# Two token groups turned in 64-token halves, seven taps one by one, token rows cut as 0–127 and 64–191

## The chip, the cores and the metric

The kernel runs on one core of a Trainium2 chip. The metric is device time in microseconds (us); the profile below is of one execution on that core. Its engines are TensorE (PE, with its weight loads PEld), VectorE (DVE), ScalarE (ACT), GpSimd (POOL) and the DMA queues that SyncE (SP) issues.

## The reference

Tokens `x` (4 × 4096 × 192) go through a dynamic convolution of 7 taps with softmax weights, 8 heads of 24 columns each, and then through a gated two-layer network with 1536 hidden columns.

```
w = softmax(weight_gen, over the 7 taps)          # per token and head
attn[s, h, :] = sum_k w[s, h, k] * x_pad[s + k, h, :]      # k = 0..6, causal
out = (silu(attn @ w_gate) * (attn @ w_val)) @ w_out       # 192 -> 1536 -> 192
```

Inputs are float32 but the arrays arrive as 64-bit floats, so the three weight matrices are rebuilt from their bits on DVE and ACT inside the kernel.

## The kernel before

The 16384 tokens are 32 groups of 4 × 128 (`NG`, `JG`; `NC` = 512 tokens). A step is one group and one of 12 slices of 128 hidden columns; groups 0 and 1 are worked in alternate steps so that the first weight slices, which are still being rebuilt, are used twice; groups 2 to 31 follow in turn. Before a group's first step its summed tokens must stand with the 192 columns on partitions. A partition has 128 rows, so the 192 are held in two tiles: `xT[g, 0]` holds rows 0–127, and `xT[g, 1]` rows 128–191, twice over (partitions 0–63 and 64–127). In the program tile 1 is "half 1". Each is split for accuracy into a rounded part (`xhi`, made by ACT, `high`) and the rest (`xlo`, by DVE, `low`).

Groups 2 to 31 (`MOVED`) are turned through DRAM. Groups 0 and 1 are needed at once, and are turned on TensorE (`summed_turn`): a matmul takes 128 tokens × 128 columns of a tap as the stationary operand and the identity as the moving one, and adds into two PSUM banks, one a half. The seven taps of a token are put together as five sums (`SUMS`): pairs (3,4) and (5,6) are added on DVE first (`product`, the line with `op=ALU.add`), the others go alone; one tap is multiplied on ACT (`scaled`, 32 small activations of 24 columns). For half 1 to be doubled, ACT copies the last 64 columns behind the 192 (the activations with `out=x[:, :, D:]`: L340, and L369 in `doubled`). So a sum costs eight matmuls of 128 × 128, two halves by four token blocks. A float32 matmul stands in the trace as two records.

An up-projection takes nine pairs of matmuls of 64 rows (`up_first`, L587 and L590, `up_second`, L599). The two of a pair use the lower and the upper 64 rows of the array and run side by side. `up_first` begins with the three pairs of half 1 alone. `up_second` waits for a handshake through POOL (`told`, `behind`).

The order of all work is written out by hand (`manual_schedule`): each engine runs its list in order. At the start PE is given a fill: 12 matmuls of the identity (`busy`, L785), then four of 128 × 64, and eight and eight of 64 rows in two shapes (L787, L791). Behind them stand the turns `t0` to `t4` of group 0, `u0` of group 1, the first step's up-projection, `u1` to `u4`, and the second step. In steps 19 to 26 ACT also multiplies a tap for group 3, four activations a step (L255; `ends` in the main body).

Of the kernel before, what the change touches and what calls it, by code (L numbers as in the profile page):

```python
# [18 lines left out]
def dynconv_glu_kernel(  # L19
# [23 lines left out]
    nc = tc.nc  # L43
# [22 lines left out]
    SUMS = {0: ((0,), (1,), (3, 4), (5, 6), (2,)), 1: ((1,), (2,), (3, 4), (0,), (5, 6))}  # L66
# [170 lines left out]
    def attention_ops(g):  # L237
# [4 lines left out]
        def mul(engine, k, into):  # L242
            src = x_t[cx][:, jx + k : jx + k + JG].rearrange("p t (h i) -> p t h i", h=H)
            w = e_t[cw][:, jw : jw + JG, :, k : k + 1].to_broadcast([P, JG, H, G])
# [70 lines left out]
    def summed_turn(g):  # L315
# [6 lines left out]

        parts = SUMS[g]

        def tap(n):
            a = {}

            def product(k, first):
                def go():
                    if first:  # L330
                        a["sum"] = att.tile([P, JG, 2 * P], F32, tag="xatt", name="tap", bufs=3)
                        mul(nc.vector, k, a["sum"][:, :, 0:D])
                    else:
                        a["other"] = att.tile([P, JG, D], F32, tag="prod", name="prod")
                        mul(nc.vector, k, a["other"])
                        x = a["sum"][:, :, 0:D]
                        nc.vector.tensor_tensor(out=x, in0=x, in1=a.pop("other"), op=ALU.add)
                    if k == parts[n][-1]:
                        x = a["sum"]
                        nc.scalar.activation(out=x[:, :, D:], in_=x[:, :, P:D], func=AF.Copy)  # L340

                return go

            def rows(t):
                if "sum" in a:
                    return a["sum"][:, t]
                return a["two"][t // 2][:, t % 2 * 2 * P : (t % 2 + 1) * 2 * P]
# [18 lines left out]
            def doubled():  # L366
# [610 lines left out]
```

## Time and profile before

| | us |
|---|---|
| median of three runs (1275.6 to 1278.42) | 1276.52 |
| the profiled execution, whole | 1276.68 |
| its span in the trace | 1274.9 |
| PE busy | 1267.9 |
| DVE busy | 1020.0 |
| ACT busy | 629.9 |

The span is what the rows add up to; 1.78 us lie around it. A busy engine is one with an instruction in flight, and matmuls overlap, so a pace is read from starts or from a row's length and count. A row of the timeline has the start, the time from the first start to the last end, engine, line, operation, output and inputs, shapes (for PE: array rows * stationary columns, then the moving operand), the count, and in brackets the idle time before it and who ended it.

### The profile page before, as it was taken

To read this page: it belongs to the slowest core of one execution; us is meant where nothing else is said; L and a number is where in the kernel's file an instruction comes from. 1 tells how busy PE (TensorE), PEld (TensorE's weight loads), DVE (VectorE), ACT (ScalarE), POOL (GpSimd) and SP (SyncE) were. 2 spreads that over 40 slices of the span, in tenths; PEclk is the share of its full clock that TensorE was granted. 3 is DMA by queue.
4 is the path that set the end of the run, shared out by engine and by line. 5 is a ranking of instruction groups with operands and counts; after the bars stand their busy time and mean duration, and the time that the engine had idled before them with its cause. 6 is when DMAs were issued, how large, how long until landed. Compare 5 with 4: busy or idle time off the path is not lost.

```text
span 1274.9 us, 31577 instructions
## 1 busy us (share of the span) xinstructions
PE 1267.9 (99%) x13280; PEld 1240.7 (97%) x13280; DVE 1020.0 (80%) x1466; ACT 629.9 (49%) x1173; POOL 0.7 (0%) x7
## 2 busy tenths in 40 slices
PE   9999999999999999999999999999999999999998
PEld 8999999999999999999999999999999999999998
DVE  8997877887877888778888777878778888778744
ACT  7656444545445454454544445454354544544443
POOL 0000000000000000000000000000000000000000
PEclk9999999999999999999999999999999999999999
DMA  5521213112121121212113121121311112111200
GB/s 163 162 76 53 74 42 107 31 27 86 30 86 43 29 92 37 79 43 82 27 34 100 38 86 42 22 78 30 94 43 47 52 42 73 43 42 32 50 18 14
DMA packets 67174, 74.89 MB, mean 59 GB/s; under 512 B 10076, under 2 KB 56412, under 8 KB 65368
## 3 DMA queue, kind: packets, MB, share of 16 engines
q1 hardware_dynamic: 66888, 72.79, 20.7%
q8 instruction: 103, 1.69, 0.6%
q14 instruction: 39, 0.32, 0.1%
q10 hardware_dynamic: 144, 0.10, 0.0%
HBM read 48.48 MB, written 24.38 MB: 57 GB/s over the span
## 4 chain that ended last, share of the span: by engine, by line
PE 99%; ACT 1%; DVE 0%; issue 0%; POOL 0%; DVEq 0%; POOLq 0%
PE up L587 25%; PE up L599 25%; PE dn L677 22%; PE up L590 21%; PE dn L686 3%; PE dn L666 2%; PE tr L352 1%; PE busy L785 0%; ACT tap L255 0%; ACT sg L613 0%; PE busy L791 0%; DVE h L629 0%; ACT L613 0%; PE busy L787 0%; ACT osb L706 0%
## 5 line engine op out<-in xcount | busy, mean ns | idle before, releaser
L677 PE MATMUL dn<-wo,hi 64*128 64x384 f32 x2880 | 564.1, 344 | 0.3 <-ACT osb L706 0.3
L686 PE MATMUL dn<-wo,lo 64*128 64x192 f32 x2880 | 501.5, 248 | 0.0
L677 PEld LDWEIGHTS dn<-wo,hi 64*128 64x128 f32 x2880 | 469.1, 184 | 6.3 <-ACT osb L706 0.7
L686 PEld LDWEIGHTS dn<-wo,lo 64*128 64x128 f32 x2880 | 445.7, 186 | 1.5 <-DVE lo L633 0.2
L630 ACT ACTIVATE hi<-h 128x512 fp32r<-128x512 f32 (+1 forms) x361 | 227.9, 631 | 349.9 <-DVE h L629 349.8
L629 DVE TENSOR_TENSOR h<-up,sg 128x512 f32<-128x512 f32 (+1 forms) x361 | 247.9, 687 | 155.6 <-ACT sg L613 155.4
L613 ACT ACTIVATE sg<-up 128x512 f32<-128x512 f32 x385 | 228.3, 593 | 263.2 <-PE up L599 252.4
L633 DVE TENSOR_TENSOR lo<-h,hi 128x512 fp32r<-128x512 f32 (+1 forms) x361 | 247.4, 685 | 82.8 <-ACT hi L630 82.7
L587 PE MATMUL up<-xhi,w_hi 64*128 64x512 f32 x768 | 222.0, 420 | 0.2 <-DVE h L629 0.2
L599 PE MATMUL up<-xhi,w_hi 64*128 64x512 f32 x768 | 221.4, 420 | 0.2
L587 PE MATMUL up<-xhi,w_lo 64*128 64x512 f32 x768 | 211.4, 393 | 0.0
L587 PE MATMUL up<-xlo,w_hi 64*128 64x512 f32 x768 | 210.3, 390 | 0.1
L590 PE MATMUL up<-xhi,w_hi 64*128 64x512 f32 x768 | 210.1, 390 | 0.0
L590 PE MATMUL up<-xhi,w_lo 64*128 64x512 f32 x768 | 210.0, 390 | 0.0
L599 PE MATMUL up<-xhi,w_lo 64*128 64x512 f32 x768 | 209.4, 389 | 0.0
L590 PE MATMUL up<-xlo,w_hi 64*128 64x512 f32 x768 | 209.3, 388 | 0.0
L599 PE MATMUL up<-xlo,w_hi 64*128 64x512 f32 x768 | 208.5, 387 | 0.0
L245 DVE TENSOR_TENSOR prod<-xt,wt 128x768 f32<-128x768 f32 x182 | 172.9, 950 | 0.0
L283 DVE TENSOR_TENSOR xatt<-xatt,prod 128x768 f32<-128x768 f32 x178 | 169.0, 949 | 0.0
L590 PEld LDWEIGHTS up<-xlo,w_hi 64*128 64x128 f32 x768 | 128.3, 184 | 3.4 <-DVE xlo L445 0.7
L590 PEld LDWEIGHTS up<-xhi,w_hi 64*128 64x128 f32 x768 | 128.0, 184 | 3.5
L590 PEld LDWEIGHTS up<-xhi,w_lo 64*128 64x128 f32 x768 | 127.9, 184 | 3.1
(69 smaller groups left out, 1362.8 us busy)
## 6 DMA issues: line engine op xcount, KB each, us to landing
xt<-in_x_dram SPq DMA_DIRECT2D x13, 1344.0 KB, 7.5
out_dram<-osb SPq DMA_DIRECT2D x117, 96.0 KB, 1.9
turned<-cut SPq DMA_DIRECT2D x116, 96.0 KB, 2.0
t<-turned SPq DMA_DIRECT2D x58, 128.0 KB, 2.7
t<-turned SPq DMA_DIRECT2D x29, 256.0 KB, 3.0
raw<-in_moe_w_out_dram SPq DMA_DIRECT2D x12, 192.0 KB, 2.7
wt<-in_weight_gen_dram SPq DMA_DIRECT2D x3, 672.0 KB, 5.7
raw<-in_moe_w_gate_dram SPq DMA_DIRECT2D x12, 128.0 KB, 2.2
```

Source lines behind the costliest of these rows:

```text
L245: engine.tensor_tensor(out=into.rearrange("p t (h i) -> p t h i", h=H), in0=src, in1=w, op=ALU.mult)
L283: nc.vector.tensor_tensor(out=a, in0=a, in1=tmp.pop(k), op=ALU.add)
L587: nc.tensor.matmul(ps, w[r, fs], m[r], start=(n == 0), stop=False)
L590: ins = nc.tensor.matmul(sums[i], w[r, i, fs], m[r], start=False, stop=False)
L599: ins = nc.tensor.matmul(sums[i], w[r, i, fs], m[r], start=False, stop=(n == len(full) - 1))
L613: nc.scalar.activation(out=sg[:, n], in_=sums[0][:, n], func=AF.Silu)
L629: nc.vector.tensor_tensor(out=h[:, n], in0=sums[1][:, n], in1=sg[:, n], op=ALU.mult)
L630: nc.scalar.activation(out=hi[:, n], in_=h[:, n], func=AF.Copy)
L633: nc.vector.tensor_tensor(out=lo[:, n], in0=h[:, n], in1=hi[:, n].bitcast(F32), op=ALU.subtract)
L666: nc.tensor.matmul(acc[g, t], hi[r, cs], wo32[r, f], start=opens and pair == 0, stop=closes and pair == 1,)
L677: nc.tensor.matmul(acc[g, t], hi[r, cs], wo[r, f].rearrange("p a d -> p (a d)"), start=opens, stop=False,)
L686: nc.tensor.matmul(acc[g, t][:, 0:D], lo[r, cs], wo[r, f, 0], start=False, stop=closes)
```

## The change

In groups 0 and 1 every tap is turned alone, so there are seven turns a group. Each is cut into 64-token halves: a matmul takes 64 tokens × 128 columns as the stationary operand and a 64 × 64 identity, and there are 16 of them, in pairs of which the lower one writes one bank and the upper one the other. A bank then has 64 tokens of each block, both halves, so that a split needs four pieces of 256 columns, two a half.

Tile 1 now holds rows 64 to 191, for all groups. No copy of columns is left; the weights' 64-row slices are loaded to fit (gate and value rows 0–63 and 128–191 in one load; rows 64–127 in `wb`), and a pair of matmuls reads the lower half of one tile and the upper half of the other. The three DMAs that bring a moved group back become two.

Group 1's tap 0 is multiplied half on ACT and half on DVE (`rest`). The last 20 matmuls of the fill go, and the 12 first stay. ACT's work for group 3 stands in steps 19 to 23 instead of 19 to 26.

```diff
-    SUMS = {0: ((0,), (1,), (3, 4), (5, 6), (2,)), 1: ((1,), (2,), (3, 4), (0,), (5, 6))}
+    SUMS = {0: (0, 1, 3, 4, 5, 6, 2), 1: (1, 2, 3, 4, 5, 6, 0)}
...
+        ps = [bank.rearrange("p (a t c) -> p a t c", a=2, t=JG) for bank in ps]
...
             def turn():
                 for half in (1, 0):
                     for t in range(JG):
-                        nc.tensor.matmul(
-                            ps[half][:, t * P : (t + 1) * P],
-                            rows(t)[:, half * P : (half + 1) * P],
-                            ident,
-                            start=(n == 0 and t == 0),
-                            stop=(n == len(parts) - 1 and t == JG - 1),
-                        )
+                        for bank, r in zip(ps, (LOW, HIGH)):
+                            nc.tensor.matmul(
+                                bank[:, half, t],
+                                rows(t)[r, half * DB : half * DB + P],
+                                ident[r, r],
+                                start=(n == 0 and half == 1 and t == 0),
+                                stop=(n == len(parts) - 1 and half == 0 and t == JG - 1),
+                            )
...
-            for r in (LOW, HIGH):
-                nc.sync.dma_start(out=t32[r, 1], in_=rows[P:D])
-            nc.sync.dma_start(out=t32[:, 0], in_=rows[0:P])
+            for half in (1, 0):
+                nc.sync.dma_start(out=t32[:, half], in_=rows[half * DB : half * DB + P])
...
+        def pieces(half, *tiles):
+            if g >= MOVED:
+                return [(ps[half], *tiles)]
+            cut = [x.rearrange("p (t l c) -> p l t c", t=JG, l=2) for x in tiles]
+            return [(ps[l][:, half], *(x[:, l] for x in cut)) for l in range(2)]
...
+        high, low = (ah[LOW], bh[HIGH]), (al[LOW], bl[HIGH])
+        mid, midlow = (bh[LOW], ah[HIGH]), (bl[LOW], al[HIGH])
         return (
-            ((wa_hi, ah), (wa_hi, al), (wa_lo, ah)),
-            ((wb_hi, bh), (wb_hi, bl), (wb_lo, bh)),
+            ((wa_hi, high), (wa_hi, low), (wa_lo, high)),
+            ((wb_hi, mid), (wb_hi, midlow), (wb_lo, mid)),
         )
...
-        bank = [ps_dn.tile([P, 2, D], F32, tag=f"dn{n}", name="busy")[:, 0] for n in range(2)]
+        bank = ps_dn.tile([P, 2, D], F32, tag="dn0", name="busy")
         for _ in range(BUSY):
-            nc.tensor.matmul(bank[0][:, 0:P], ident, ident, start=True, stop=True)
-        for _ in range(4):
-            nc.tensor.matmul(bank[0][LOW, 0:P], ident[:, LOW], ident, start=True, stop=True)
-        for cols in (slice(0, P), LOW):
-            for _ in range(4):
-                for to, r in zip(bank, (LOW, HIGH)):
-                    nc.tensor.matmul(to[cols, LOW], ident[r, cols], ident[r, r], start=True, stop=True)
+            nc.tensor.matmul(bank[:, 0, 0:P], ident, ident, start=True, stop=True)
...
-        for n, op in enumerate(aside[1:]):
-            ends.setdefault(19 + n, []).append(op)
+        for n, op in zip((19, 20, 20, 21, 22, 22, 23, 23), aside[1:]):
+            ends.setdefault(n, []).append(op)
```

On PE, from the program's start to the first up-projection, in the kernel before (tr are the PSUM banks of group 0, tr_181 and tr_180 those of group 1, up an up-projection's):

```order
L785 MATMUL busy<-ident 128x128 x12
L787 MATMUL busy<-ident 64x128 x4
L791 MATMUL busy<-ident 128x64 x8
L791 MATMUL busy<-ident 64x64 x8
L352 MATMUL tr<-ident,tap 128x128 x40
L352 MATMUL tr_181<-ident,tap 128x128 x4
L352 MATMUL tr_180<-ident,tap 128x128 x4
L587 MATMUL up<-xhi,w_hi 128x512 x2
```

and in the changed one (tr_159 and tr_160 are group 1's banks; eight such pairs stand there):

```order
L792 MATMUL busy<-ident 128x128 x12
L344 MATMUL tr<-ident,tap 128x64 x112
L344 MATMUL tr_159<-ident,tap 128x64
L344 MATMUL tr_160<-ident,tap 128x64
...
L594 MATMUL up<-xhi,w_hi 128x512 x2
L594 MATMUL up<-xlo,w_hi 128x512 x2
L594 MATMUL up<-xhi,w_lo 128x512 x2
```

The 20 smaller matmuls of the fill are gone; 40 matmuls of group 0 became 112, and the 8 of group 1's first turn became 16.

On ACT, from group 1's last turns to its second step, before:

```order
L255 ACTIVATE tap<-xt,wt 128x24 x8
L369 ACTIVATE tap<-tap 128x2x64 x2
L502 ACTIVATE e<-e,exp_bias 128x576
L340 ACTIVATE tap<-tap 128x4x64
L438 ACTIVATE xhi<-tr_181 128x512
L438 ACTIVATE xhi<-tr_180 128x512
L553 ACTIVATE w_hi<-w 128x3x128
```

and now:

```order
L256 ACTIVATE tap<-xt,wt 128x24 x4
L507 ACTIVATE e<-e,exp_bias 128x576
L438 ACTIVATE xhi<-tr_159 128x4x64
L438 ACTIVATE xhi<-tr_160 128x4x64
L438 ACTIVATE xhi<-tr_159 128x4x64
L438 ACTIVATE xhi<-tr_160 128x4x64
L558 ACTIVATE w_hi<-w 128x3x128
```

The copies are gone, and two activations out of the banks became four, each of which reads half of a bank.

On ACT, where groups 0 and 1 end (osb takes the finished sums out of their banks dn), before:

```order
L476 ACTIVATE wo<-wo_93 128x192
L255 ACTIVATE tap<-xt,wt 128x24 x4
L613 ACTIVATE sg<-up 128x512
L630 ACTIVATE hi<-h 128x512
L255 ACTIVATE tap<-xt,wt 128x24 x4
L706 ACTIVATE osb<-dn_522 128x2x192
L706 ACTIVATE osb<-dn_523 128x2x192
L613 ACTIVATE sg<-up 128x512
L630 ACTIVATE hi<-h 128x512
L255 ACTIVATE tap<-xt,wt 128x24 x4
L706 ACTIVATE osb<-dn_570 128x2x192
L706 ACTIVATE osb<-dn_571 128x2x192
```

and now:

```order
L481 ACTIVATE wo<-wo_93 128x192
L256 ACTIVATE tap<-xt,wt 128x24 x8
L620 ACTIVATE sg<-up 128x512
L637 ACTIVATE hi<-h 128x512
L713 ACTIVATE osb<-dn_622 128x2x192
L713 ACTIVATE osb<-dn_623 128x2x192
L620 ACTIVATE sg<-up 128x512
L637 ACTIVATE hi<-h 128x512
L713 ACTIVATE osb<-dn_670 128x2x192
L713 ACTIVATE osb<-dn_671 128x2x192
```

No tap activation stands in front of the osb copies any more; they moved to the steps ahead.

## Rows read from the trace of the kernel before

**Rows 1.** The page: the span, and the chain that ended last, by engine.
```profile
span 1274.9 us, 31577 instructions
...
PE 99%; ACT 1%; DVE 0%; issue 0%; POOL 0%; DVEq 0%; POOLq 0%
```

**Rows 2.** Stages: PE, PEld, DVE, ACT, POOL busy us, granted clock, DMA.
```profile
1.39:6.80 5.41, 5.41 (x24) 5.20 (x24) 3.59 (x9) 3.35 (x8) 0.00 (x0) 1.00 0.90 287
...
9.55:20.66 11.11, 11.11 (x100) 10.87 (x96) 9.50 (x16) 9.40 (x38) 0.00 (x0) 1.00 0.68 209
...
40.00:60.00 20.00, 20.00 (x205) 19.17 (x204) 19.11 (x35) 13.46 (x31) 0.00 (x0) 1.00 0.51 154
```

**Rows 3.** Timeline of PE, the fill and the turns behind it.
```profile
1.39 5.49 PE L785 MATMUL busy<-ident 128*128 128x128 f32 x24 [1.39 <-POOL ident masks.py:199]
...
7.90 1.11 PE L791 MATMUL busy<-ident 64*128 64x64 f32 x16
8.94 0.68 PE L791 MATMUL busy<-ident 64*64 64x64 f32 x16
...
9.55 11.19 PE L352 MATMUL tr<-ident,tap 128*128 128x128 f32 x96
```

**Rows 4.** Timeline of PE at 8.72 to 8.76, three neighbouring pairs.
```profile
8.51 0.50 PE L791 MATMUL busy<-ident 64*128 64x64 f32 x6
```

**Rows 5.** The line L791: ns min/median/max of one, first and last start, shapes.
```profile
L791 PE MATMUL busy<-ident x32: 218/270/320, 7.9 to 9.4; 64*128 64x64 f32 x16, 64*64 64x64 f32 x16
```

**Rows 6.** Timeline of DVE and ACT ahead of the first turn.
```profile
5.99 2.69 DVE L245 TENSOR_TENSOR tap<-xt,wt 128x768 f32<-128x768 f32 x3
...
7.28 0.40 ACT L340 ACTIVATE tap<-tap 128x256 f32<-128x256 f32 x1
```

**Rows 7.** Timeline of PE, from the first step's end to the second's.
```profile
22.57 0.51 PE L599 MATMUL up<-xhi,w_hi 64*128 64x512 f32 x2
...
23.48 2.05 PE L352 MATMUL tr<-ident,tap 128*128 128x128 f32 x16
...
26.18 5.68 PE L352 MATMUL tr<-ident,tap 128*128 128x128 f32 x48 [0.65 <-ACT tap L340]
31.79 0.50 PE L587 MATMUL up<-xhi,w_hi 64*128 64x512 f32 x2
...
34.12 0.51 PE L599 MATMUL up<-xhi,w_hi 64*128 64x512 f32 x2
```

**Rows 8.** Timeline of ACT and DVE: splits of tokens and of weights.
```profile
20.52 0.55 DVE L559 TENSOR_TENSOR w_lo<-w,w_hi 128x384 fp32r<-128x384 f32 x1
...
31.00 0.60 ACT L438 ACTIVATE xhi<-tr 128x512 fp32r<-128x512 f32 x1 [1.86 <-PE tr L352]
...
31.63 0.69 DVE L445 TENSOR_TENSOR xlo<-tr,xhi 128x512 fp32r<-128x512 f32 x1 [0.64 <-ACT xhi L438]
```

**Rows 9.** Timeline of PE, where groups 0 and 1 end.
```profile
118.25 0.28 PE L686 MATMUL dn<-wo,lo 64*128 64x192 f32 x2
118.80 0.82 PE L677 MATMUL dn<-wo,hi 64*128 64x384 f32 x2 [0.28 <-ACT osb L706]
...
120.96 0.25 PE L686 MATMUL dn<-wo,lo 64*128 64x192 f32 x1
121.05 0.35 PE L677 MATMUL dn<-wo,hi 64*128 64x384 f32 x1
...
125.87 0.25 PE L686 MATMUL dn<-wo,lo 64*128 64x192 f32 x1
126.41 0.49 PE L587 MATMUL up<-xhi,w_hi 64*128 64x512 f32 x1 [0.19 <-DVE h L629]
```

**Rows 10.** Timeline of ACT, in those steps and some ahead.
```profile
101.89 0.60 ACT L613 ACTIVATE sg<-up 128x512 f32<-128x512 f32 x1 [1.01 <-PE up L599]
...
117.28 0.91 ACT L255 ACTIVATE tap<-xt,wt 128x24 f32<-128x24 f32 x4
118.26 0.87 ACT L706 ACTIVATE osb<-dn 128x384 f32<-128x384 f32 x2
```

More of the change, by code (lines that the diff above doesn't have):

```diff
@@ L326, in tap, with product @@
             a = {}
[L328 to L342, printed above, removed]
+            k = parts[n]
+            def product():
+                a["sum"] = att.tile([P, JG, 2 * P], F32, tag="xatt", name="tap", bufs=3)
+                mul(nc.vector, k, a["sum"][:, :, 0:D])
             def rows(t):
                 if "sum" in a:
-                    return a["sum"][:, t]
-                return a["two"][t // 2][:, t % 2 * 2 * P : (t % 2 + 1) * 2 * P]
+                    return a["sum"][:, t, 0:D]
+                return a["two"][t // 2][:, t % 2 * 2 * P : t % 2 * 2 * P + D]
             def turn():
@@ L364, in begun, with rest @@
                 ]
-            def doubled():
-                for x in a["two"]:
-                    x = x.rearrange("p (t d) -> p t d", t=2)
-                    nc.scalar.activation(out=x[:, :, D:], in_=x[:, :, P:D], func=AF.Copy)
-            if parts[n][0] in SCALED.get(g, ()):
-                return [begun, *scaled(parts[n][0], rows), doubled], turn
-            return [product(k, m == 0) for m, k in enumerate(parts[n])], turn
+            def rest():
+                x = a["two"][1].rearrange("p (t d) -> p t d", t=2)[:, :, 0:D]
+                mul(nc.vector, k, x, slice(2, JG))
+            if k in SCALED.get(g, ()):
+                aside = scaled(k, rows)
+                if g:
+                    aside = [*aside[: len(aside) // 2], rest]
+                return [begun, *aside], turn
+            return [product], turn
         return ps, [tap(n) for n in range(len(parts))]
@@ L404, in places @@
                     )
-                for i, half, to in ((4, 1, 0), (5, 1, 1), (4, 1, 2), (5, 1, 3), (0, 0, 0), (1, 0, 1), (2, 0, 2), (3, 0, 3)):
+                for i, half, to in ((2, 1, 0), (3, 1, 1), (4, 1, 2), (5, 1, 3), (0, 0, 0), (1, 0, 1), (2, 0, 2), (3, 0, 3)):
                     nc.sync.dma_start(
@@ L434, in split_ops @@
         hi = [xts.tile([P, NC], F32R, tag=f"xhi{half}", name="xhi") for half in range(2)]
+        def pieces(half, *tiles):
[3 more added lines that the diff above has]
+            return [(ps[l][:, half], *(x[:, l] for x in cut)) for l in range(2)]
         def high(half):
             def go():
-                nc.scalar.activation(out=hi[half], in_=ps[half], func=AF.Copy)
+                for data, to in pieces(half, hi[half]):
+                    nc.scalar.activation(out=to, in_=data, func=AF.Copy)
             return go
@@ L444, in go @@
                 lo = xts.tile([P, NC], F32R, tag=f"xlo{half}", name="xlo")
-                nc.vector.tensor_tensor(
-                    out=lo, in0=ps[half], in1=hi[half].bitcast(F32), op=ALU.subtract
-                )
+                for data, high, to in pieces(half, hi[half], lo):
+                    nc.vector.tensor_tensor(
+                        out=to, in0=data, in1=high.bitcast(F32), op=ALU.subtract
+                    )
                 xT[g, half] = hi[half], lo
@@ L599, in up_second @@
                 ins = nc.tensor.matmul(
-                    sums[i], w[r, i, fs], m[r], start=False, stop=(n == len(full) - 1)
+                    sums[i], w[r, i, fs], m[1 - i], start=False, stop=(n == len(full) - 1)
                 )
```

47 lines of the change are left out of this document (26 added, 21 removed).

## The prediction

> **What bounds the kernel now.** I read the page first: PE is on 99% of the chain that ended last, in a span of 1274.9 us [rows 1]. A microsecond of PE time added or taken is therefore a microsecond of the whole wherever PE has no gap. The table by stages says where that holds: from 9.55 to 20.66, the first turns, PE is busy for all 11.11 us, and from 40 to 60 for 20.00 of 20.00, though DVE is there close behind with 19.11 [rows 2]. So the change, nearly all of it ahead of 40 us, is settled by PE's own list up to the second step, and then by the places where PE waits.
>
> PE's timeline comes next [rows 3]. The 24 records of the first fill take 5.49 us, 0.23 each, and the 96 of L352, of the same shape, 11.19, or 0.117 each. The granted clock reads 1.00 in both stretches [rows 2]; by the pace the first stood at 1.2 GHz and the second at 2.4 GHz, and what went before the rise was the fill itself. The first turn begins at 9.55, right behind the fill's last part.
>
> **The change part by part.** All sums are made against the profiled execution, 1276.68 us whole; the median of the runs, 1276.52, is 0.16 lower.
>
> *The shorter fill.* Before, the data of the first turn were ready when ACT's copy ended, at 7.28 + 0.40 = 7.68 [rows 6], but PE was held by the fill until 9.55. Now the copy is gone and the first product is enough: DVE's three take 2.69 from 5.99, so the first ends at about 6.9 [rows 6]; with 0.1 for the handover PE starts at 7.0. The twelve fill matmuls that stay end at 1.39 + 5.49 = 6.88 [rows 3], just ahead. Gain 2.55. Its bound on the other side: if the first turn still runs at the lower level, it takes 16 × 0.23 = 3.7 instead of 1.85, so that 0.7 is left of the gain.
>
> *The turns.* A sum was 8 matmuls, 16 records of L352. A tap is now 16 matmuls of 64 rows, 8 pairs, each in two records: 16 pairs of records. Is a pair cheaper than one full pass? The fill that is removed holds this very shape, 64 rows by 128 stationary columns with 64 moving: 16 records, 8 pairs, from 7.90, with 1.11 to the last end [rows 3]. Three neighbouring pairs take 0.50 [rows 4]; less one record's own 0.27 [rows 5] that is two steps of 0.115. Between the two rows, (1.11 - 0.50) / 5 = 0.122, with a slow first step in it. So a pair takes what a full 128 × 128 pass takes, 0.117. The second shape of L791, 64 by 64, is the nearest row on the other side: (0.68 - 0.22) / 7 = 0.066 a pair [rows 3, 5]; it has the same 64 moving columns and half the stationary ones, which says that it is the 128 stationary columns that cost 0.115. The changed kernel keeps 128 of them, so I take 0.115, with 0.112 to 0.122 as the range of this case. A turn is then 16 × 0.115 = 1.84, as a sum was 16 × 0.117 = 1.87, and there are 14 for 10. Four more turns: +7.4 (7.1 to 7.8).
>
> The Trainium skill bears on this with two pages. TensorE: Matmul & The Clock Gate, section LDWEIGHTS (loading the stationary operand), says that a load's time goes by the stationary columns and not by the rows; by its formula 128 columns are an estimated 107 ns, and the trace agrees with its 115. TensorEngine Tiling (Array Packing), section Theoretical Speedup, promises up to twice the speed for a dimension of 64 or less; by it a turn would be 0.92, which is a rival below. The row that has this shape speaks for the first.
>
> *Adds and copies that go.* Four adds leave DVE and every copy leaves ACT. Neither sets the time ahead of the first step, since PE has no gap there, and a product of 0.9 [rows 6] now feeds a turn of 1.84. What does go is the one wait for a copy, 0.65 ahead of 26.18 [rows 7]: -0.65.
>
> *The splits.* Each half's split becomes two pieces of 256 columns. The row of 512 takes 0.60 on ACT and 0.69 on DVE [rows 8]; the copy of 256 took 0.40 [rows 6]; so a piece is 0.30 to 0.40 on ACT, and 0.35 to 0.45 on DVE. Both banks are complete only with the last pair of the last turn, and the first pair of the up-projection now reads both tiles, so that it waits for all four ACT pieces, 1.2 to 1.6. For group 0 the turn u0, 1.84, lies between and covers them. DVE's four pieces and the weights' rest, 0.55 [rows 8], end later than that by about 0.2, which I count: +0.2 (0 to 0.5). For group 1 nothing stands between: u6 is followed by the second step at once. Before, half 1 was finished four matmuls early, ACT began its split at 31.00 and PE went on at 31.79, with no gap behind the turn's 26.18 + 5.68 = 31.86 [rows 7, 8]. Now PE stands for four pieces and a handover, +1.5. From the first pair to the handshake it took 34.12 - 31.79 = 2.33 [rows 7], in which it waited for both xlo; now it waits once, -0.2. Together +1.3 (1.0 to 1.7).
>
> *One shape.* Turns and up-projections now have the same 64-row shape, where before the array went from one to another at three places. At such a change the trace has 8.94 where 8.51 and three steps of 0.115 would give 8.85 [rows 3, 4], and about as much again in the step behind it. Three times 0.15: -0.45 (-0.6 to 0).
>
> *Where groups 0 and 1 end.* PE waits at 118.80 for the osb copies on ACT, and at 126.41 for h [rows 9]. L677 follows L686 by 0.09 elsewhere (120.96, 121.05); here they are 0.55 and 0.54 apart, so each place loses about 0.45. Ahead of osb on ACT stands L255 with 0.91 [rows 10]. With that moved, osb is early by more than the loss, and so is all of ACT that follows. The steps that take the work over have room: the wait at 101.89 is 1.01 [rows 10] and the second four activations add 0.82 to 0.91. -0.9 (-0.9 to 0).
>
> *All other groups.* Rows of tile 1 and one DMA less per group change no matmul's shape or number. The two of a pair now read different tiles; no row shows that, and as each reads its own 64 partitions in any case I price it at nothing. Groups' splits end two steps ahead of their use, which covers the tile that is now needed at once.
>
> Sum: -2.55 + 7.4 - 0.65 + 0.2 + 1.3 - 0.45 - 0.9 = +4.35, so 1281.0 for the profiled execution's own time, and 1280.9 against the median. With all low ends it is -2.55 + 7.1 - 0.65 + 0 + 1.0 - 0.6 - 0.9 = +3.4, with all high ends -0.7 + 7.8 - 0.65 + 0.5 + 1.7 + 0 + 0 = +8.65: against the median, 1279.9 to 1285.2 is this case's own range.
>
> **The rivals.**
>
> *The halves really run at twice the pace, and the kernel gets faster.* Then a turn costs 16 × 0.066 = 1.06, and DVE takes over as the limit: from 9.55 to 20.66 it was busy for 9.50 of 11.11 [rows 2], and two adds and a product of about 0.9 leave that stretch, so that the first step could begin some 3 us earlier; in group 1 DVE has about as much to do as before, so the rest cancels against the 1.3 of the splits. With the 0.9 and 0.45: about 1276.7 - 3.5 = 1273. It decides at a pair below 0.08. For it: the two of a pair do run beside each other. Against it: the row of this shape [rows 4]. Chance 0.09.
>
> *The clock falls back during the turns.* For it: no row shows a long stretch of this shape, and PE now stands for 0.1 ahead of the first turn. At the lower level a pair takes 0.23 and a turn 3.7, so 14 turns cost up to 26 us more; with half of them so, about 1294. Against it: the records of L791 were at the upper level, and 11 us of L352 behind them stayed there [rows 3]. The Trainium skill, TensorE: Matmul & The Clock Gate, section Part 4: PE-mode transpose, says that the upper level does not engage for its transpose mode; these are plain matmuls with an identity, and L352, used likewise, held its pace. Chance 0.08.
>
> *The late start is given back.* DVE is busy for 19.11 of 20 us from 40 on [rows 2]. If it and not PE sets the pace there, a PE that comes five microseconds late catches up, and what is left is the 0.9: about 1275.8, within 0.2%. Against it: PE is busy for 20.00 of the same 20. Chance 0.09.
>
> **How the numbers follow.** My forecast has 0.74. 0.2% of this time is 2.55 us, about what a measurement of this kernel can tell from no change, so slower begins at 1279.1 and faster ends at 1274.0. The forecast lies above 1279.1 but for its lowest end and the scatter of the runs (1275.6 to 1278.4 before), for which I take off 0.08. Slower: 0.66 + 0.08 = 0.74. Faster: 0.09, and 0.02 of the third rival. Same: 0.07 + 0.08 = 0.15. The range goes down from the case's own 1279.9 by the scatter and part of the third rival to 1277.0, and up to 1286.0; the first rival, the second and most of the third lie outside.
>
> **What would show it.** The first turn's records start at 7.0, not 9.55; their pairs follow each other in 0.115 (wrong if under 0.09, and at 0.23 the clock has fallen); fourteen turns fill about 25.8 us of PE; the second step's first pair stands some 1.5 behind the last turn and at about 37, not 31.79; no wait for osb near 124. The prediction is wrong if PE has a gap between the turns of group 0, for then something other than PE sets them, or if a step of group 2 or later takes another time than before.

## The result and the profile after

The changed kernel takes 1283.54 us (median of six runs, 1282.62 to 1283.86), the kernel before 1276.42 beside it (1275.6 to 1278.42): a ratio of 1.0052, interval 1.0039 to 1.0065. It is slower by 7.1 us, where 4.4 were forecast. The profiled execution took 1283.22, 6.54 more than that of before.

The page of the changed kernel, its span and its chain by engine [rows 1 before]:

```profile
span 1281.4 us, 32005 instructions
...
PE 98%; DVE 1%; SPq 0%; DMA 0%; issue 0%; ACT 0%; DVEq 0%; POOLq 0%
```

SP's queue and the DMA are on the chain now, and DVE's share has gone from 0% to 1%. Its timeline of PE, from the fill to the third step (start, length, engine, line, operation, tiles, count, idle time ahead and who ended it), answers to [rows 3] and [rows 7]:

```profile
1.39 5.34 PE L792 MATMUL busy<-ident 128*128 128x128 f32 x24 [1.39 <-POOL ident masks.py:199]
6.86 7.36 PE L344 MATMUL tr<-ident,tap 64*128 64x64 f32 x128
14.78 5.58 PE L344 MATMUL tr<-ident,tap 64*128 64x64 f32 x96 [0.56 <-DVE tap L246]
20.66 2.00 PE L344 MATMUL tr<-ident,tap 64*128 64x64 f32 x32 [0.30 <-DVE tap L246]
22.47 0.48 PE L594 MATMUL up<-xhi,w_hi 64*128 64x512 f32 x2
...
25.39 10.83 PE L344 MATMUL tr<-ident,tap 64*128 64x64 f32 x192
36.96 1.34 PE L594 MATMUL up<-xhi,w_hi 64*128 64x512 f32 x2 [0.74 <-ACT xhi L438]
...
39.29 1.05 PE L597 MATMUL up<-xhi,w_hi 64*128 64x512 f32 x2
...
44.01 0.39 PE L597 MATMUL up<-xhi,w_hi 64*128 64x512 f32 x2
...
46.25 0.53 PE L594 MATMUL up<-xhi,w_hi 64*128 64x512 f32 x2
```

The turns are as forecast: the first at 6.86 for 7.0, a pair every 0.112 (10.83 for 96 pairs) for 0.115. That the second step then stands at 36.96, for about 37, is luck: the part on the prediction has the sum. Two things were not forecast. PE waits twice for DVE between the turns of group 0. And the pairs of the second step are slow: 1.05 for two records, against 0.39 from 44.01 on. The table by stages (PE, PEld, DVE, ACT, POOL busy us with counts, granted clock, DMA share, GB/s; [rows 2] before) says why:

```profile
6.86:14.22 7.36, 7.36 (x128) 7.22 (x128) 3.47 (x5) 3.17 (x15) 0.00 (x0) 1.00 0.37 114
...
25.39:36.20 10.81, 10.81 (x194) 10.68 (x190) 5.77 (x9) 2.08 (x6) 0.00 (x0) 1.00 0.24 76
...
36.96:43.60 6.64, 6.53 (x24) 4.06 (x26) 3.22 (x8) 2.55 (x7) 0.00 (x0) 0.52 0.30 90
44.00:60.00 16.00, 16.00 (x164) 14.19 (x162) 14.95 (x27) 8.36 (x14) 0.00 (x0) 1.00 0.40 121
```

For 6.64 us the granted clock is 0.52, the lower of the two levels, 1.2 GHz. PE had done 10.8 us of turns at the upper level, and then waited 0.74.

The waits in group 0 are read on DVE and on SP's queue. First DVE of the changed kernel, then SP, whose column of length is the time that an issue takes:

```profile
13.40 0.46 DVE L495 TENSOR_SCALAR e<-raw 128x576 int32<-128x576 int32 x1 [3.53 <-DMA raw<-in_moe_w_out_dram]
```

```profile
3.91 2.77 SPq L468 DMA_DIRECT2D raw<-in_moe_w_gate_dram  x1
...
9.07 1.96 SPq L463 DMA_DIRECT2D raw<-in_moe_w_val_dram  x1
11.07 2.95 SPq L468 DMA_DIRECT2D raw<-in_moe_w_gate_dram  x1
```

The same of the kernel before, DVE and then SP:

```profile
10.46 0.46 DVE L490 TENSOR_SCALAR e<-raw 128x576 int32<-128x576 int32 x1
```

```profile
3.54 0.57 SPq L469 DMA_DIRECT2D raw<-in_moe_w_gate_dram  x1
...
7.04 0.47 SPq L469 DMA_DIRECT2D raw<-in_moe_w_gate_dram  x1
```

DVE's first work on the weights starts at 13.40 and not at 10.46, after 3.53 of waiting for a DMA (that of `w_out`, the last of the slice's five), and the product of the fifth turn stands behind it. SP takes 2 to 3 us for issues that took 0.5. The slow ones are not the first loads of two blocks themselves (L463, 0.70 and 0.52 at 2.59 and 3.34) but what stands in the queue behind such loads: the second of a slice's two (9.07), and the 64-row load behind both (L468, 3.91 and 11.07). What the DMA engines moved in the first 30 us (busy tenths and GB/s in 40 slices), changed kernel:

```profile
DMA  0049698711379521111246998211111366111211
GB/s 0 0 119 244 198 369 353 306 70 48 126 160 333 208 67 46 48 46 48 78 139 163 320 350 298 80 48 49 51 46 46 124 167 214 46 46 45 68 47 46
```

It falls again and again to between 45 and 51 GB/s and one tenth of busy time. Before, no slice was below 125 GB/s from the start of the loads to 18 us, where they first paused.

Where groups 0 and 1 end, two places answer to [rows 9]: the first pair of step 25 (the second of group 2) and of step 40, 15 steps on, in the changed kernel and then in the one before (there with the fourth step's first pair above them):

```profile
120.33 0.53 PE L594 MATMUL up<-xhi,w_hi 64*128 64x512 f32 x2
...
168.87 0.41 PE L594 MATMUL up<-xhi,w_hi 64*128 64x512 f32 x1
```

```profile
37.82 0.53 PE L587 MATMUL up<-xhi,w_hi 64*128 64x512 f32 x1
...
111.90 0.52 PE L587 MATMUL up<-xhi,w_hi 64*128 64x512 f32 x1
...
162.16 0.41 PE L587 MATMUL up<-xhi,w_hi 64*128 64x512 f32 x1
```

48.54 against 50.26: the stretch is 1.7 shorter, where 0.9 was forecast. At the fourth step's first pair the changed kernel is 8.43 behind (46.25 against 37.82), at the end 6.54.

The split of group 1, on ACT and DVE, answers to [rows 8]:

```profile
36.25 1.21 ACT L438 ACTIVATE xhi<-tr 128x256 fp32r<-128x256 f32 x4 [8.58 <-PE tr L344]
...
37.22 1.42 DVE L446 TENSOR_TENSOR xlo<-tr,xhi 128x256 fp32r<-128x256 f32 x4 [4.04 <-ACT xhi L438]
```

The four ACT pieces take 1.21 and the first DVE piece starts 0.97 behind the first of them, so `xlo` is complete only at 38.64, and the second step waits for it too.

### The profile page after: what moved, and what is told of

The parts are those of the page before. It is cut to its first block, busy times and chain, and to the rows that moved or that the text cites. A ratio compares the mean times of both kernels' runs of the same rounds, so it can differ in the third digit from the quotient of the medians.

```text
span 1281.4 us, 32005 instructions
## 1 busy us (share of the span) xinstructions
PE 1274.0 (99%) x13528; PEld 1226.2 (96%) x13528; DVE 1017.6 (79%) x1467; ACT 623.9 (49%) x1149; POOL 0.7 (0%) x7
## 4 chain that ended last, share of the span: by engine, by line
PE 98%; DVE 1%; SPq 0%; DMA 0%; issue 0%; ACT 0%; DVEq 0%; POOLq 0%
PE up L594 25%; PE up L606 25%; PE up L597 20%; PE dn L684 19%; PE dn L693 6%; PE dn L673 2%; PE tr L344 1%; DMA raw<-in_moe_w_out_dram 0%; SPq L468 0%; DVE tap L246 0%; SPq L463 0%; SPq L154 0%; SPq L138 0%; DVE m L521 0%; DVE w L546 0%
## 5 line engine op out<-in xcount | busy, mean ns | idle before, releaser
L684 PE MATMUL dn<-wo,hi 64*128 64x384 f32 x2880 | 580.3, 344 | 0.0
L693 PE MATMUL dn<-wo,lo 64*128 64x192 f32 x2880 | 518.2, 248 | 0.0
L684 PEld LDWEIGHTS dn<-wo,hi 64*128 64x128 f32 x2880 | 488.1, 184 | 9.7
L693 PEld LDWEIGHTS dn<-wo,lo 64*128 64x128 f32 x2880 | 456.5, 186 | 0.5 <-DVE lo L640 0.2
L594 PE MATMUL up<-xhi,w_hi 64*128 64x512 f32 x768 | 229.9, 420 | 0.7 <-ACT xhi L438 0.7
L606 PE MATMUL up<-xhi,w_hi 64*128 64x512 f32 x768 | 229.4, 421 | 0.2
L594 PE MATMUL up<-xhi,w_lo 64*128 64x512 f32 x768 | 220.0, 394 | 0.0
L594 PE MATMUL up<-xlo,w_hi 64*128 64x512 f32 x768 | 218.8, 391 | 0.0
L597 PE MATMUL up<-xhi,w_hi 64*128 64x512 f32 x768 | 218.4, 390 | 0.0
L597 PE MATMUL up<-xhi,w_lo 64*128 64x512 f32 x768 | 218.2, 390 | 0.0
L597 PE MATMUL up<-xlo,w_hi 64*128 64x512 f32 x768 | 217.2, 387 | 0.0
L606 PE MATMUL up<-xhi,w_lo 64*128 64x512 f32 x768 | 217.2, 390 | 0.0
L606 PE MATMUL up<-xlo,w_hi 64*128 64x512 f32 x768 | 216.4, 387 | 0.0
L597 PEld LDWEIGHTS up<-xhi,w_hi 64*128 64x128 f32 x768 | 134.5, 185 | 6.3
L597 PEld LDWEIGHTS up<-xlo,w_hi 64*128 64x128 f32 x768 | 134.7, 185 | 5.8
L597 PEld LDWEIGHTS up<-xhi,w_lo 64*128 64x128 f32 x768 | 134.0, 184 | 6.2
```

What stands on the lines that cost most here:

```text
L594: nc.tensor.matmul(ps, w[r, fs], x, start=(n == 0), stop=False)
L597: ins = nc.tensor.matmul(sums[i], w[r, i, fs], m[i], start=False, stop=False)
L606: ins = nc.tensor.matmul(sums[i], w[r, i, fs], m[1 - i], start=False, stop=(n == len(full) - 1))
L684: nc.tensor.matmul(acc[g, t], hi[r, cs], wo[r, f].rearrange("p a d -> p (a d)"), start=opens, stop=False,)
L693: nc.tensor.matmul(acc[g, t][:, 0:D], lo[r, cs], wo[r, f, 0], start=False, stop=closes)
```

## The experiments

The theory after this profile had four parts: the turns and the split's wait cost what was forecast; the new weight loads are slow and hold DVE; the clock falls behind group 1's turns; and group 3's new place is worth about twice its price. The rivals: the wait and not the shape of the turns lets the clock fall; the late weights are its cause; DVE and not PE sets the turns. All were timed beside the kernel before, which took 1276.2 to 1276.4.

### The weight loads by themselves

The changed kernel, its loads of two blocks cut into two of 64 rows:

```diff
-            queue.dma_start(
-                out=raw[:, n * P : (n + 1) * P].rearrange("p n w -> p (n w)"),
-                in_=w.rearrange("(b r) f -> b r f", r=DB)[0::2, :, fs].bitcast(I32),
-            )
+            for r, at in ((LOW, 0), (HIGH, P)):
+                queue.dma_start(
+                    out=raw[r, n * P : (n + 1) * P].rearrange("p n w -> p (n w)"),
+                    in_=w[at : at + DB, fs].bitcast(I32),
+                )
```

> The changed kernel, with the gate and value rows 0-63 and 128-191 loaded by two 64-row DMAs each instead of one that takes both blocks. Theory (the two-block load is slow to move): the exponent on DVE, which waited 3.53 us for weights and began at 13.40, begins at 9.8 to 10.5; PE has no gap ahead of the turns at 14.78 and 20.66, so the first step's first pair comes at about 21.6 instead of 22.47, and the whole is about 0.9 us faster than the changed kernel, 1282.6. Rival (the loads are late for their place in the queue or their bytes): two DMAs more per slice make the exponent later still, 13.4 or more, and the time is the same or longer. Both: the clock still falls at the second step.

Measured: 1281.77, ratio 1.0041 (1.0028 to 1.0053), 1.8 below the changed kernel. Its DVE and PE:

```profile
9.84 0.45 DVE L496 TENSOR_SCALAR e<-raw 128x576 int32<-128x576 int32 x1
```

```profile
21.23 0.48 PE L595 MATMUL up<-xhi,w_hi 64*128 64x512 f32 x2
```

No wait for a DMA, no gap between the turns of group 0, and the first step comes 1.24 earlier (21.23 for 22.47). Half a microsecond of that is given back at once, since PE now waits for `xlo` in the first step: group 1's turns start at 24.68 for 25.39, 0.7 earlier. The rest of the 1.8 is a clock that falls a little later: the granted clock is 1.00 from 36.30 to 38.30 and 0.54 from 38.30 to 42.00. One of the five runs took 1280.3 at a mean clock of 1.0, where the other four have 0.997 or 0.998, so in that one the fall seems to have stayed out. The loads are one cause, and not what makes the clock fall: with no late weights it still falls in four runs of five. The bytes are the same as in the changed kernel. The DMA engines' busy tenths in the first 30 us, with these loads:

```profile
DMA  0049699998797343069898546514433674544560
```

The Trainium skill has this rule, on a page that the prediction didn't use: DMA: Bandwidth & Descriptors, section Why a DMA increments its semaphore by 16 and not by 1, says that a DMA runs on the largest number of engines up to 16 that divides the slowest dimension of both its sides. The new load's slowest dimension on the DRAM side is 2, so by the rule it has two engines. The trace agrees: 16 of the 40 slices stand at one tenth of busy time in the changed kernel, 15 of them at 45 to 51 GB/s, and one slice with the 64-row loads.

### The clock, held by a fill

The changed kernel with ten 128 × 128 matmuls of the identity behind group 1's last turn, in the time in which PE waits:

```diff
+        def filled():
+            for _ in range(10):
+                nc.tensor.matmul(bank[:, 0, 0:P], ident, ident, start=True, stop=True)
...
-        todo[0] += w1[2:4] + [high1, high0, *w1[4:6], low1, low0] + w1[6:9]
+        todo[0] += [filled] + w1[2:4] + [high1, high0, *w1[4:6], low1, low0] + w1[6:9]
```

> The changed kernel, with ten 128 by 128 matmuls of the identity between group 1's last turn and the second step, where PE stood. Theory (the clock falls because PE waits there): the granted clock stays at 1.00 from 37 to 44 us, the second and third steps' lengths go from 5.78 and 3.51 to about 3.4 and 2.9, and the time from 1283.5 to about 1280.6. Rival (the clock falls because of ten microseconds of turns in the 64-row shape, wait or no wait): the granted clock falls to about 0.5 in spite of the fill, and the time is 1283.5 or more.

Measured: 1281.28, ratio 1.0036 (1.0023 to 1.0048), 2.3 below the changed kernel, though PE does 2.4 us more work. The fill and the second step behind it in this kernel, and the table's row for the stretch:

```profile
35.83 2.50 PE L814 MATMUL busy<-ident 128*128 128x128 f32 x20
```

```profile
38.26:43.00 4.74, 4.62 (x41) 3.61 (x42) 3.19 (x8) 1.63 (x3) 0.00 (x0) 1.00 0.26 81
```

The granted clock stays at 1.00, and in all five runs the mean clock is 0.999 or 1.0. The second step and the third take 2.57 and 2.92 instead of 5.78 and 3.51.

### A wait behind full passes

The kernel before, with ACT held by five idle copies ahead of group 1's split:

```diff
+        def held():
+            for _ in range(5):
+                nc.scalar.activation(out=scratch, in_=ps1[1][:, 0 : 2 * P], func=AF.Copy)
...
-        todo[0] += [high1, high0, *w1[4:7], low1, low0] + w1[7:9]
+        todo[0] += [held, high1, high0, *w1[4:7], low1, low0] + w1[7:9]
```

> The kernel before, with five idle activations that read a finished bank ahead of group 1's split, so that PE, after 128 by 128 turns, stands for about 1.2 us ahead of the second step. Theory (a wait there is enough for the clock to fall): the granted clock falls to about 0.5 for some 6 us from 33 us on, and the time is the wait and about 3 more, 1280.7. Rival (it also takes the 64-row turns ahead): the clock stays at 1.00, and only the wait is added, 1277.7.

Measured: 1278.08, ratio 1.0015 (1.0006 to 1.0024). The second step's first pair and the stretch behind it:

```profile
32.91 0.51 PE L588 MATMUL up<-xhi,w_hi 64*128 64x512 f32 x2 [1.73 <-ACT xhi L439]
```

```profile
32.91:38.00 5.09, 4.76 (x40) 3.48 (x40) 4.24 (x8) 2.73 (x6) 0.00 (x0) 1.00 0.24 75
```

PE waits 1.73, more than twice the changed kernel's 0.74, and the clock holds. In this trace only the wait is paid. Two of the eleven runs took 1280.05 and 1280.63 at a mean clock of 0.998, the other nine 1277.2 to 1279.0 at 0.999 or 1.0; no run of the kernel before beside it has less than 0.999, so the clock may have fallen in those two, of which there is no trace. The changed kernel shows 0.997 or 0.998 in all six of its runs. So a wait, even a longer one, seldom does it here by itself; what the engine did before it counts.

### The fill ahead of the last turn

The fill as above, moved to the front of the last turn: `[u5, q6[5], filled, u6]` in place of `[u5, q6[5], u6]`, and nothing behind it.

> The changed kernel with the ten 128x128 matmuls of e2_fill put ahead of the last turn of group 1 instead of behind it: the wait for the ACT pieces behind the last turn (0.74) stays as it was, and so does a turn of 64-row halves ahead of it, but the 10.8 us of such turns are cut at 9. Theory (the long stretch of 64-row turns, together with the wait, lets the clock fall; a short one does not): granted clock 1.00 from the second step on, 20 x 0.12 = 2.4 more PE time and about 3.3 less in the second and third step: 1282.6. Rival (any wait of 0.7 behind a 64-row turn lets it fall): granted clock about 0.5 in the second step as in the changed kernel, 2.4 more: 1285.9.

Measured: 1286.35, ratio 1.0093 (1.0078 to 1.0108): the rival's number. The wait and the stretch behind it:

```profile
39.32 1.04 PE L594 MATMUL up<-xhi,w_hi 64*128 64x512 f32 x2 [0.74 <-ACT xhi L438]
```

```profile
41.10:47.60 6.50, 6.39 (x27) 4.57 (x29) 3.32 (x7) 1.63 (x3) 0.00 (x0) 0.50 0.37 115
```

2.4 us of full passes between the turns don't keep the clock up through a wait of 0.74 behind the last of them. Two of the six runs took 1290.5 and 1292.1 at a mean clock of 0.991 to 0.993, more than this fall; the next experiments show where that can come from.

### Full passes, then a wait, in the changed kernel

The fill behind the last turn, with five idle ACT copies too (the lines are set against the kernel with that fill):

```diff
-        todo[0] += [filled] + w1[2:4] + [high1, high0, *w1[4:6], low1, low0] + w1[6:9]
+        todo[0] += [filled] + w1[2:4] + [held, high1, high0, *w1[4:6], low1, low0] + w1[6:9]
```

> The changed kernel with the ten 128x128 matmuls behind group 1's last turn (e2_fill) and with five idle ACT copies of 256 columns ahead of the split, as in e3_held, so that PE waits again, for about 0.9 us, but now behind full passes and not behind a 64-row turn. Theory (what counts is the shape that ran directly ahead of the wait): granted clock 1.00 from the second step on, and only the wait is paid, with about 0.4 for the late xlo: 1281.28 + 0.9 + 0.4 = 1282.6. Rival (any wait in this place lets the clock fall, because the 10.8 us before it were 64-row turns): granted clock about 0.5 in the second step, 3 more: 1285.6.

Measured: 1286.11, from 1283.01 to 1289.49, in two kinds: three runs of 1283.0 to 1283.3 at a mean clock of 0.999 to 1.0, and three of 1288.9 to 1289.5 at 0.994 to 0.995. The profiled run is one of the latter, and its loss is elsewhere: in group 0, behind one of the waits for the slow weights. Its PE, and the table by stages:

```profile
14.86 12.70 PE L345 MATMUL tr<-ident,tap 64*128 64x64 f32 x128 [0.64 <-DVE tap L247]
```

```profile
16.80:29.00 12.20, 12.20 (x110) 11.92 (x110) 7.50 (x16) 5.64 (x24) 0.00 (x0) 0.50 0.37 115
44.60:48.00 3.40, 3.05 (x14) 1.54 (x16) 3.15 (x8) 1.92 (x5) 0.00 (x0) 1.00 0.52 156
```

At the second step, the place in question, the clock is 1.00, and the three undisturbed runs are 0.4 to 0.7 above the theory's 1282.6. That speaks for it, but weakly: PE's wait behind the fill came out at 0.30 and not 0.9. What it adds is that the changed kernel's group 0 stands at an edge: behind about 7.4 us of turns a wait of 0.56 passed in the changed kernel, and one of 0.64 cost some 6 us here.

### The converse in the kernel before

16 pairs of 64-row matmuls behind the full-pass turns of group 1, and eight idle copies:

```diff
+        def rows64():
+            for _ in range(16):
+                for to, r in zip(bank, (LOW, HIGH)):
+                    nc.tensor.matmul(to[:, LOW], ident[r], ident[r, r], start=True, stop=True)
...
-            for _ in range(5):
+            for _ in range(8):
...
-        todo[0] += [held, high1, high0, *w1[4:7], low1, low0] + w1[7:9]
+        todo[0] += [rows64, held, high1, high0, *w1[4:7], low1, low0] + w1[7:9]
```

> The converse in the kernel before: e3_held with 16 pairs of 64-row matmuls by an identity (64 x 128 stationary, 64 moving, the shape of the changed kernel's turns, 1.85 us) between group 1's last turn and the wait, and eight idle ACT copies instead of five, so that PE waits for about 1.15 behind them. All turns are full passes as before. Theory (the shape directly ahead of the wait): the clock falls, granted clock about 0.5 in the second step and its pairs 0.43 apart: 1278.08 + 1.24 for the later copies + 3.0 = 1282.3. Rival (the changed kernel's turns of 10 us are needed, or its other splits): granted clock 1.00: 1279.3.

Measured: 1279.56, ratio 1.0025 (1.0016 to 1.0035), the rival's number, but it settles nothing. The PE rows of this kernel:

```profile
30.96 3.79 PE L816 MATMUL busy<-ident 64*128 64x64 f32 x64
34.56 0.49 PE L588 MATMUL up<-xhi,w_hi 64*128 64x512 f32 x2
```

Each matmul makes two records, 64 in all; the added passes took 3.79 and not 1.85, and filled the wait that was to follow them. There is no gap ahead of 34.56, so no wait was tried. Whether two microseconds of 64-row passes are enough, and whether it is their rows or their 64 moving columns, stays open.

### Five sums instead of seven

The changed kernel with the 64-row loads, and with the sums of two taps again, `{0: ((0,), (1,), (3, 4), (5, 6), (2,)), 1: ((1,), (2,), (3, 4), (5, 6), (0,))}`, added on DVE and turned in halves without copies.

> The changed kernel with the 64-row weight loads of e1_loads64 and with five sums a group again instead of seven (two sums of two taps, added on VectorE), turned in 64-row halves all the same, still without copies. So each group has two turns fewer. Theory: a turn costs 16 pairs of 0.112, 1.79 us of PE, wherever PE has no gap, and the four more turns are the whole reason that the change is slower: 4 x 1.79 = 7.2 below e1_loads64's 1281.77, so 1274.6; if the clock then also stays at the upper level behind group 1's five turns (9.0 us of them in place of 10.8 behind the first step), 1.2 less, 1273.4. Rival: VectorE, which gets its four adds of 0.96 back and two pieces more in each split, sets the pace of the turns, PE has gaps of 0.5 to 1.0 before turns with an add: 1276 to 1278.

Measured: 1281.3, ratio 1.0042 (1.003 to 1.0054). Neither number came. Its turns of group 0, and the stretches by stage:

```profile
6.92 5.64 PE L350 MATMUL tr<-ident,tap 64*128 64x64 f32 x96
13.62 10.27 PE L350 MATMUL tr<-ident,tap 64*128 64x64 f32 x96 [1.06 <-DVE tap L339]
```

```profile
14.50:26.50 12.00, 12.00 (x101) 10.99 (x100) 8.84 (x17) 4.85 (x21) 0.00 (x0) 0.50 0.54 157
```

With two adds back, DVE is late for the fourth turn by 1.06, as the rival says, and behind that wait the clock falls for at least 12 us: three turns take 10.27 for 5.4. It falls again in the second step, behind four turns of group 1 (7.25 us) and a wait of 0.75: 0.53 from 37.60 to 40.60. The mean clock is 0.991 to 0.994 in all five runs. The falls cost about what the saved turns give. So this way back to five sums gains nothing as it stands (a fill in its waits was not tried), and the fall of the clock is shown at a second place, after 5.6 us of turns.

### Both repairs

The changed kernel with the 64-row loads and the fill behind the last turn.

> The changed kernel with both repairs: 64-row weight loads (e1_loads64) and the ten 128x128 matmuls behind the last turn (e2_fill). If the two effects are separate, 1283.54 - 1.8 - 2.3 = 1279.4; if the part of e1_loads64's gain that came from the clock falling later is the same microseconds as e2_fill's, 1.24 + 2.3 less: 1280.0. Either way still slower than before (1276.4), by about the 4.4 that were forecast less the 1.0 more that group 3's steps gave: that is what the turns cost. Rival: the two are one effect (the late weights cause the fall of the clock), then no better than 1281.3.

Measured: 1280.62, ratio 1.0036 (1.0024 to 1.0048), 2.9 below the changed kernel and 4.4 above the one before. All five runs lie within 0.3 and have a mean clock of 0.999 or 1.0. It is 0.7 better than the fill alone and 1.15 better than the loads alone, 1.1 short of the sum of both; 0.6 of overlap was expected, and the first step's wait for `xlo`, which the loads bring with them, is the 0.5 beyond that.

### Two turns fewer

> e7_mended without the sixth turn of group 0 and of group 1 (their products are still made, but not turned, so that the fifth tap listed last but one is missing from both groups' sums): two turns fewer, in a kernel where PE has no gap and the clock stays up. Theory (a turn costs its 16 pairs of 0.112 on PE and nothing hides them): 2 x 1.79 = 3.58 less than 1280.62: 1277.0. Rival (VectorE's products, or the weights' conversion, would set the pace at once): 1278.5 or more, with gaps of PE between the turns.

The edit takes `[t5]` and `u5` out of the two lists, so that this kernel leaves one tap out of the sums of either group. Measured: 1277.59, 3.0 below the kernel with both repairs; 3.58 was expected. At the third step the two traces are 3.5 apart (37.10 against 40.60). A gap ahead of the last turn of group 0 is new:

```profile
18.71 2.00 PE L344 MATMUL tr<-ident,tap 64*128 64x64 f32 x32 [0.64 <-DVE tap L246]
```

So turns are paid on PE, and with one fewer DVE already sets part of group 0's pace, as the rival says. Here a wait of 0.64 passed without a fall: the outcome at that edge isn't fixed by the length of the wait. Two of the eleven runs, 1278.8 and 1278.9, have a mean clock of 0.998, and no trace.

### Half the fill

With both repairs, and five matmuls in the fill.

> e7_mended with five in place of ten 128x128 matmuls behind group 1's last turn: 10 records of 0.117, 1.2 us, which just cover the wait for the ACT pieces. Theory (the full passes matter, not their number): the clock stays at 1.00 and PE comes 1.0 to 1.2 earlier: 1279.5. Rival (so short a fill does not hold the clock through what is left of the wait): the fall comes back, 1282 or more.

Measured: 1280.21, ratio 1.003 (1.0019 to 1.0041), 0.4 below the ten. The clock is 1.00 from 36.80 to 42.00. PE is at the second step at 36.76 instead of 38.03, but then waits for DVE's `xlo` pieces and takes 3.56 for it instead of 2.57. The rows of that wait and of the fourth step:

```profile
37.99 0.50 PE L595 MATMUL up<-xlo,w_hi 64*128 64x512 f32 x1 [0.17 <-DVE xlo L446]
...
43.24 0.52 PE L595 MATMUL up<-xhi,w_hi 64*128 64x512 f32 x2
```

The second half of the long fill thus ran in time that PE would have waited.

### Group 3's place by itself

The kernel before with that one line:

```diff
-        for n, op in enumerate(aside[1:]):
-            ends.setdefault(19 + n, []).append(op)
+        for n, op in zip((19, 20, 20, 21, 22, 22, 23, 23), aside[1:]):
+            ends.setdefault(n, []).append(op)
```

> The kernel before, with ACT's taps for group 3 in steps 19 to 23 as in the changed kernel, and nothing else. The prediction's term: PE's waits at 118.80 and 126.41 go, 0.9 less, 1275.6. What the distance between the two traces says: it shrinks by 1.93 from the third step to the end, in the steps from 26 on, so 1274.5. If both are wrong and the gain came from the other parts of the change, no difference.

Measured: 1274.56 (11 runs), ratio 0.9986 (0.9978 to 0.9995): 1.9 faster than before. The stretch that took 50.26 takes 48.58 here:

```profile
111.19 0.53 PE L587 MATMUL up<-xhi,w_hi 64*128 64x512 f32 x2
...
159.77 0.41 PE L587 MATMUL up<-xhi,w_hi 64*128 64x512 f32 x1
```

Besides the steps of [rows 9] (0.7 and 0.4), four later ones lose 0.6 together before the change, and nothing after it. Those have no idle row of their own.

### The short fill on top

That kernel with the first fill cut to its twelve 128 × 128 matmuls.

> The kernel before with group 3's steps (e4_group3) and with the first fill cut to its twelve 128x128 matmuls, which end at 6.88; turns, copies and weights as before. Theory (the fill holds the first turn): the first turn starts when its copy ends, 7.7 instead of 9.55, the rise of the clock comes in time, and 1.85 is saved: 1274.56 - 1.85 = 1272.7. Rival (VectorE, busy for 9.5 of 11.1 us of the first turns, and the copies set the pace): the turns get gaps, the first step stays near 20.7: 1274.5.

Measured: 1275.58, ratio 0.9996 (0.9988 to 1.0005), no better. Its turns:

```profile
7.61 5.62 PE L352 MATMUL tr<-ident,tap 128*128 128x128 f32 x48 [1.48 <-ACT tap L340]
14.14 5.62 PE L352 MATMUL tr<-ident,tap 128*128 128x128 f32 x48 [0.91 <-ACT tap L340]
19.70 0.50 PE L587 MATMUL up<-xhi,w_hi 64*128 64x512 f32 x2
```

The first turn starts at 7.61, as expected, and 0.91 is waited for later, since DVE and the copies set the pace, as the rival says; and from 143 to 151 two steps lose 0.8 that they did not lose without this edit. Waits of 1.48 and 0.91 around full passes leave the clock at 1.00.

Of all these, the kernel before with group 3's place moved is the best: faster than both kernels, by 0.14% and by 0.7%.

## Why the prediction was right in its sign and short in its size

The direction and its main reason hold. Up to the fourth step the sum was -2.55 + 7.4 - 0.65 + 0.2 + 1.3 - 0.45 = +5.25; the traces give +8.43. For group 1 the rows are taken from the end of its last turn (36.22 in the changed kernel, 35.51 with half the fill) to the fourth step's first pair:

| term | forecast | measured | from |
|---|---|---|---|
| shorter fill | -2.55 | -2.69 | 6.86 against 9.55 |
| turns and one shape | +6.95 | +6.4 | 14.31 (with the 64-row loads, 6.92 to 21.23) + 10.83 against 11.11 + 2.05 + 5.61 |
| the wait for the ACT copy | -0.65 | -0.65 | no such wait left |
| split of group 0 | +0.2 | +0.1 | 25.39 - 22.47 against 23.48 - 20.66; +0.6 with the weights in time |
| split of group 1 | +1.3 | +1.7 | 7.73 with a held clock (half the fill, 35.51 to 43.24) against 6.03 (31.79 to 37.82) |
| weights late in group 0 | 0 | +1.3 | 22.47 - 6.86 against 14.31 |
| clock in the second and third step | 0 | +2.3 | 10.03 (36.22 to 46.25) against those 7.73; the fill alone gave 2.3 |
| where groups 0 and 1 end | -0.9 | -1.9 | 8.43 less 6.54; by itself 1276.43 - 1274.56 |

*The turns.* A pair costs what a full pass costs, so four more turns are on PE in full; the experiment with two turns fewer gives 3.0 of 3.58. Over-sized by some 0.6: a turn is 1.79 and not 1.84, and the forecast put the four new turns at that price without the gain on the ten old ones; by its own rows 14 × 1.84 - 10 × 1.87 = 7.1 and not 7.4. The rows do not show the one shape apart from the turns. The rival of twice the pace is out with 0.112 against its 0.08. *The splits:* group 1's came out at the upper end of its range. Of the second step's first pair one matmul starts at 36.96 and the other at 37.51, behind the last of ACT's pieces, so the forecast's +1.5 for that wait holds, nearly. But it let the wait for `xlo` shrink by 0.2, and half the fill shows that DVE's last piece comes after ACT's and is what ends the waiting: with PE kept busy through the wait for ACT, the step still waits for `xlo` until 37.99, 2.5 behind the last turn.

*The step of the prediction that failed: the weights.* The prediction has no term for the new weight loads; the one DMA fewer that it names is that of the moved groups. That issues behind these loads take 2 to 3 us instead of 0.5, and that the last load of a slice holds DVE for 3.53, was not asked. The prediction had named the sign of it, a gap of PE between the turns of group 0, and by that sign its account of group 0 was wrong. The 64-row loads show the cause: 1.24 at the first step. That the second step stood at 36.96 for about 37 all the same is luck: 1.3 of late weights stands against turns that are 0.6 cheaper and a first wait of 0.74 where 1.5 was put.

*The other such step: the clock.* Its rival was half right. It had the fall during the turns, at 0.08, and dismissed it with full passes that held. The turns did hold; the fall came behind them, with the wait that the prediction itself had put there at +1.5. Nothing in it asked what that wait does to the clock. The fill shows the size, 2.3, and the held copies show that the same place, with a longer wait behind full passes, cost nothing of the kind in nine runs of eleven. The Trainium skill, TensorE: Matmul & The Clock Gate, section HAM oscillation — how this bites in real kernels, puts the fall down to waits for data between groups of matmuls. In these traces the longer wait, 1.73 behind full passes, left the clock at 1.00 and the shorter, 0.74 behind 64-row turns, did not, so the length of the wait alone does not tell.

*The late start given back* is out: the distance stays at 8.4 from 46 us to 117, through the stretch where DVE is busiest, and at 6.5 to 6.7 from 200 us to the end. *Where groups 0 and 1 end* had the right mechanism, and its size was read from the two places with an idle row alone; with four more steps, of groups 2 and 3, it is twice that. So its other sign of being wrong, a step of group 2 or later that takes another time, came too: those four are 0.1 to 0.3 shorter.

The two terms that were missed, +3.6, the split of group 1, +0.4, group 3's place, -1.0, the turns, -0.6, and -0.2 from the fill and the split of group 0 make 6.5 of the 4.35. The profiled executions differ by that much and the medians by 7.1. Either lies inside the range, but the range reached that far up for other terms, a first turn at the lower level above all, so that it holds the result is luck as well. Part of the difference between the two is the fill: in this profile of the kernel before the first turn stands at 9.55, in three kernels that begin as it does at 8.73 to 8.86. The kernel with both repairs is 4.4 above before, as forecast, but by differences that cancel: its two splits cost some 0.9 more than forecast, and group 3's place gives 1.0 more.

## What to carry to other kernels

Before passes of 64 rows are put in place of full ones, look for the waits behind them: in this kernel a wait of 0.74 behind such passes cost 2.3 us beyond itself, while one of 1.73 behind full passes mostly cost itself alone, and five full matmuls in the wait were enough to keep the clock up. When a load is rearranged, look at the outermost dimension of its two sides, and at the issues that stand behind it in its queue. An edit that rides along should be timed by itself: here the slower change held a line worth 1.9 us.

## What the runs showed of the hardware

- A pair of 64 × 128 passes with 64 moving columns steps at 0.112, a full 128 × 128 pass with 128 at 0.117: half the rows and half the moving columns save next to nothing.
- While loads with an outermost dimension of 2 were in flight the DMA engines moved 45 to 51 GB/s, and the issue behind such a load took up to 2.95 us in the first 30; cut in two, the loads issue in about 0.6 each (1.21 to 1.24 for two, once 2.15).
- In the traces the clock fell behind 64-row turns and waits of 0.64 (once), 0.74, 0.75 and 1.06, for 3 to 13 us; it held behind full passes and waits of 0.65 to 1.73, and behind 64-row turns and waits of 0.30, 0.56 and once 0.64. Runs of one kernel can differ in it: by their mean clocks the fall stayed out in one of five runs with the 64-row loads, and may have come in two of eleven behind full passes. Which feature of the turns decides stays open.
- The first fill of 24 records took from 4.32 to 5.49 in profiles of the same instructions, so that the first turn stands at 9.55 in the kernel before and at 8.85 in the one with group 3's place, which begins alike: differences of 0.7 between two single traces that begin there are not the edit's.
